# Sparse attention and a mixer: weights loaded ahead of a batch, one batch turned on TensorE, the last tile stored in halves

## The chip, the cores and the metric

One core of a Trainium2 chip runs the whole program. TensorE (PE) multiplies, VectorE (DVE) and ScalarE (ACT) move and transform data, GpSimd (POOL) and SyncE (SP) issue most of the transfers, and ScalarE issues some as well. The metric is the device time of one execution in microseconds (us). It is given as the median of the runs, with the lowest and the highest; the profile is of one more execution.

## The reference

Eight batches, eight heads, 576 positions, 64 numbers a head. Attention is local (32 positions to each side) plus eight global positions that see everything and are seen by everything. Its output goes through a mixer over positions and one over channels.

```python
scores = scale * np.matmul(q, k.transpose(0, 1, 3, 2))
mask = np.abs(pos[:, None] - pos[None, :]) <= window
mask = mask | is_global[:, None] | is_global[None, :]
attn = softmax(np.where(mask, scores, -1e9))
x = np.matmul(attn, v)            # heads side by side: (8, 576, 512)
xt = x.transpose(0, 2, 1)
h = np.maximum(xt @ w_tok1, 0.0) @ w_tok2
u = x + h.transpose(0, 2, 1)
h2 = np.maximum(u @ w_ch1, 0.0) @ w_ch2
return u + h2
```

## The kernel before, in words

**Tiles.** A batch has 576 positions: four full tiles (tau 0 to 3) of 128 and a rest of 64. The rests of an even batch and the odd batch after it share one tile, tau 4. Everything that TensorE reads is float16; it sums into eight banks of float32.

**Steps of one batch b.** The loads of q and k (`load_qk`, L502; their rests `load_rest`, L511) and v (`load_v`, L519) bring float32; casts (`cast_qk` L528, `cast_v` L540) make float16, and `shift_v` (L549) a shifted copy of v, called vod. q and k have to be turned so that the head's 64 numbers lie on partitions: for batches 0 to 2 TensorE does it (`turn_pe`, L560, and `rest_pe`, L581), for batches 3 to 7 a transposing DMA into `raw`, issued by SP, and a VectorE copy out of it (`turn_dma`, L637). `scores` (L658) multiplies, ScalarE takes the exponentials into e, VectorE masks them (L689). The global keys and queries are gathered for four batches at once by indirect DMAs of POOL (`f_gather`, L484) into g_q and g_k, cast and turned in `glob_rows` (L614). `glob_keys`, `glob_sums` and `values` (L696, L715, L731) end in x. `token1` and `token2` (L797, L815) are the mixer over positions, with the result a1 between them; their end is u, added by VectorE at L834 (L837 for the rest, into `ul`). `turn_u` (L840) turns u into uT: for batches 0 to 2 by four transposes of TensorE (L848) and a copy (L850) for each of four tiles, for batches 3 to 7 by a transposing DMA of SP (L853). The shared rest is always turned by a DMA (L843). `chan1` (L862) makes twelve pieces of b1 from wc1 and uT, `chan1l` (L872) the same for the shared rest, `chan2` (L887) multiplies b1 by wc2, in two or three parts of one sum; VectorE adds u at L903 and writes one of three buffers `osb`, and a store takes it to the output (L906 from POOL, or from SP for the last batch; L909 for the shared rest, two stores of 64 rows on SP).

**What sets the order.** No order is written by hand. The program first lists operations with `op`: the engines that may run each with a cost, a priority, what it reads and writes, and for a DMA its work, its packets and its latency. Then `run` (L119) plays the list against these costs: it picks the engine and the operation that can start first, prefers low priorities among those that start close together, and issues the instruction there and then. So the costs and the due times in the code set the order of each engine's instructions, and each engine later works in that order. SP, ACT and POOL have a planned ring of 4096 packets each (L116), and eight semaphores are planned for POOL's transfers and eight for those of SP and ACT together (L131): the ninth transfer of a group waits for the first to land. `warm` (L282) puts multiplications of zeros into planned gaps of TensorE before planned time 34.

**Around the change.** POOL's queue carries, after batch 0: the weights w1 and w2, the gather of g_k, batch 1's q and k, then the channel weights wc1 in three pieces and wc2 in three (`f_wc1` L473, `f_wc2` L479), batch 1's v, all of batch 2, and the second gather. Their priorities stand in L922 to L988. SP's queue carries batch 0, then the loads of batches 3 to 7 between the transposing DMAs; ACT issues v of batches 3 to 7 (L946). Of the last batch, `chan2` for tau 4 comes last of all: two parts of six multiplications of 512 columns, one addition of 512 columns, two stores on SP.

Of the kernel before, what the change touches and what calls it, by code (L numbers as in the profile page):

```python
# [15 lines left out]
P = 128  # L16
# [11 lines left out]
def kernel(  # L28
# [90 lines left out]
    def run(free, look, hop, warm_until):  # L119
# [73 lines left out]
        while ready:  # L193
# [52 lines left out]
            if o["dma"]:  # L246
                work, size, lag, packets = o["dma"]
                q = "A" if e == "K" else e
                drain(min(f, min(free[x] for x in "GSA")))
                f = land(q, f, work, size, i)  # L250
                filled[q].append((f, packets))
                f += lag
                lanes["G" if e == "G" else "S"].append(f)
                f += o["late"] + (LATE if st > 36.0 else 0.3)
# [632 lines left out]
    def chan2(b, tau, pri):  # L887
        i, key = b % 2, ("o", b, tau)
        last = tau == NT - 1
        js = [range(0, 4), range(4, 8), range(8, 12)] if b == 0 else [range(0, 6), range(6, 12)]  # L890
        for part, jr in enumerate(js):
            def f(e, jr=jr):
# [29 lines left out]
    def loads(b, n0=0):  # L922
# [8 lines left out]
            return  # L931
        if b < PEB:
            if b == 1:
                pl = -173.9
            load_rest(b, pl, [("G", 0.73)], [n0] if b == 1 else ())
            for h in range(0, H, 4):
                for ti in range(2):
                    load_qk(b, ti, slice(h, h + 4), pl + 1 + h / 2 if b > 1 else pl + 0.1 + h / 100, [("G", 0.88)], [n0] if b == 1 else ())
            if b > 1:
                load_v(b, pl + 6, [("G", 0.87)])  # L940
        else:
            load_rest(b, pl, [("S", 0.65)])
            for h in range(0, H, 4):
                for ti in range(2):
                    load_qk(b, ti, slice(h, h + 4), pl + 1 + h / 2, [("S", 0.5)])
            load_v(b, pl + 6, [("A", 0.6)])  # L946

    def casts(b):
# [7 lines left out]
    for b in range(B):  # L956
# [17 lines left out]
            op([("G", 0.75)], -16, f_pads2(1), w=[("x", 1, NT - 1), ("lf", 1)])  # L974
        if b < 2:
            for ti in range(2):
                op([("G", 2.7)], (-115 if ti == 0 else -174.2) if b == 0 else 70, f_gather(b, ti), r=["idx"], w=[("g32", b, ti)], dma=(0.1, 256, 1.7, 256), late=0.0 if b or ti else 2.3,
                   behind=[] if b == 0 and ti == 0 else [n2])
        casts(b)
        cast_v(b, ca - 20, [("A", 0.52), ("V", 0.57)] if b < 2 else [("A", 0.52)])  # L980
# [31 lines left out]
        for tau in range(NT):  # L1012
            token2(b, tau, ca + tau)
            if tau < NT - 1 or b % 2:
                turn_u(b, tau, ca + tau + 2, b < 3)
        if b and b % 2 == 0:
            chan2(b - 1, NT - 1, base + 24)
        for j in range(NJ):
# [40 lines left out]
```

## Time and profile before

| | us |
|---|---|
| median of 3 runs | 317.6 |
| lowest and highest of them | 314.32 and 320.36 |
| the profiled execution, its own time | 314.6 |
| its span, first to last instruction | 312.9 |
| TensorE busy in it | 292.0 |
| VectorE, ScalarE, GpSimd busy | 186.8, 180.5, 60.5 |
| mean granted TensorE clock | 0.987 of full speed |

The span leaves out 1.7 us of the profiled execution's time. In the views that the prediction shows, a row of the timeline gives the start in us, the duration, the engine with the line of the code and the tile written and read, how many instructions were merged into it, and in brackets the idle time of that engine just before it and what ended it. A table by stage gives for each stretch the busy time of each engine with its count of instructions, then the granted clock, the share of the DMA engines' time that was busy, and the rate. Ends of matmuls are modelled, so the distance from one start to the next tells more than a duration.

### The profile page before, as it was taken

How to read it: one execution, taken by the hardware profiler on the slowest of the kernel's cores; microseconds unless marked ns; L12 is line 12 of the kernel's file. 1: busy time of each engine (PE TensorE's matmuls, PEld its weight loads, DVE VectorE, ACT ScalarE, POOL GpSimd, SP SyncE). 2: the span in 40 equal slices, each digit the busy share in tenths (PEclk: the TensorE clock that was granted, in tenths of full speed). 3: DMA queues.
4: the chain of work that ended last, by engine and by line, in shares of the span. 5: the costliest groups of instructions: out<-in, count | busy, mean ns of one | idle time of the engine just before them, and what ended most of it. 6: DMA issues, size and time to landing. Idle time of an engine off the chain costs nothing.

```text
span 312.9 us, 7276 instructions
## 1 busy us (share of the span) xinstructions
PE 292.0 (93%) x2943; PEld 154.4 (49%) x2943; DVE 186.8 (60%) x410; ACT 180.5 (58%) x325; POOL 60.5 (19%) x109
## 2 busy tenths in 40 slices
PE   6979889997999979988999998999999999999994
PEld 4755545454474434533456444544555445444641
DVE  7789667569686674876675846964543357230021
ACT  4864895377987758841989376733742083305500
POOL 8589635632001100002000110002000200020000
PEclk9989999999999979999999999999999999999998
DMA  6989999999999999999979999924003211051013
GB/s 183 255 129 287 208 222 222 287 243 234 214 212 220 194 267 318 118 190 221 325 114 176 203 313 189 159 50 136 36 0 63 89 53 37 12 140 69 2 67 102
DMA packets 94660, 51.31 MB, mean 164 GB/s; under 512 B 73698, under 2 KB 89954, under 8 KB 94626
## 3 DMA queue, kind: packets, MB, share of 16 engines
q1 hardware_dynamic: 62480, 26.49, 40.3%
q0 software_dynamic: 8704, 18.45, 24.0%
q10 hardware_dynamic: 23442, 5.90, 11.1%
q8 instruction: 23, 0.38, 0.5%
q14 instruction: 11, 0.09, 0.1%
HBM read 36.11 MB, written 9.44 MB: 146 GB/s over the span
## 4 chain that ended last, share of the span: by engine, by line
PE 58%; DMA 26%; ACT 5%; DVE 5%; issue 2%; SPq 2%; POOL 1%; POOLq 0%; ACTq 0%; DVEq 0%
PE bank L895 22%; PE bank L866 21%; DMA lv<-in_v_dram 8%; DMA raw<-qk 6%; DMA lq<-in_q_dram 5%; PE bank L821 4%; DMA g_q<-in_q_dram,idx_i 3%; PE bank L673 3%; PE bank L803 2%; DMA lk<-in_k_dram 2%; PE bank L878 2%; ACT qk L534 2%; ACT vsh L546 2%; DVE osb L903 2%; PE bank L753 1%
## 5 line engine op out<-in xcount | busy, mean ns | idle before, releaser
L866 PE MATMUL bank<-uT,wc 128*128 128x512 f16 x384 | 94.0, 384 | 6.4 <-DVE osb L903 2.3
L895 PE MATMUL bank<-wc,b 128*128 128x512 f16 x384 | 88.3, 379 | 2.9 <-DVE osb L903 2.2
L858 ACT ACTIVATE b<-bank 128x512 f16<-128x512 f32 x88 | 52.5, 617 | 38.3 <-PE bank L866 38.3
L683 ACT ACTIVATE e<-bank 128x648 f16<-128x648 f32 x64 | 42.7, 737 | 30.0 <-PE bank L673 29.8
L895 PEld LDWEIGHTS <-b 128*128 128x128 f16 x384 | 36.7, 98 | 45.9 <-issue 4.2
L866 PEld LDWEIGHTS <-wc 128*128 128x128 f16 x384 | 35.2, 98 | 48.5 <-issue 8.7
L906 POOL DMA_DIRECT2D out_dram<-osb x28 | 16.1, 574 | 203.1 <-DVE osb L903 203.0
L903 DVE TENSOR_TENSOR osb<-u,bank 128x512 f32<-128x512 f16 x32 | 21.9, 686 | 45.3 <-PE bank L895 41.5
L546 ACT CAST vsh<-lv 128x512 f16<-128x512 f32 (+3 forms) x44 | 26.5, 620 | 9.7 <-DMA uT<-u 5.3
L689 DVE TENSOR_TENSOR e<-e,masku 128x1296 f16<-128x1296 f16 x28 | 23.3, 831 | 13.7 <-ACT e L683 13.2
L834 DVE TENSOR_TENSOR u<-x,bank 128x512 f16<-128x512 f16 x30 | 18.7, 681 | 15.0 <-PE bank L821 14.8
L781 DVE TENSOR_TENSOR x<-bank,rr 128x512 f16<-128x512 f32 x32 | 22.1, 691 | 1.1
L821 PE MATMUL bank<-a,w 128*128 128x512 f16 x80 | 20.1, 379 | 0.5 <-DVE a L809 0.3
L534 ACT CAST qk<-lq 128x512 f16<-128x512 f32 x26 | 16.2, 626 | 4.5 <-DMA lq<-in_q_dram 2.0
L803 PE MATMUL bank<-x,w 128*128 128x512 f16 x64 | 18.7, 379 | 0.0
L673 PEld LDWEIGHTS <-kT 64*128 64x128 f16 x576 | 11.2, 97 | 14.4 <-issue 13.6
L534 ACT CAST qk<-lk 128x512 f16<-128x512 f32 x27 | 16.9, 631 | 1.8 <-DMA lk<-in_k_dram 1.8
L654 DVE COPY qT<-raw 128x512 f16<-128x512 f16 x20 | 12.0, 602 | 7.2 <-DMA raw<-qk 7.1
L753 PEld LDWEIGHTS <-e 128*64 128x64 f16 x576 | 16.1, 116 | 0.1
L740 PE MATMUL bank<-rf,lf 128*64 128x264 f16 x144 | 15.6, 293 | 0.5 <-DVE rf L726 0.5
L753 PE MATMUL bank<-vsh,e 128*64 128x66 f16 x320 | 16.0, 199 | 0.0
L673 PE MATMUL bank<-qT,kT 64*128 64x72 f16 x576 | 15.4, 198 | 0.0
(164 smaller groups left out, 333.6 us busy)
## 6 DMA issues: line engine op xcount, KB each, us to landing
out_dram<-osb POOLq DMA_DIRECT2D x28, 256.0 KB, 4.3
lq<-in_q_dram SPq DMA_DIRECT2D x11, 512.0 KB, 6.4
lk<-in_k_dram SPq DMA_DIRECT2D x11, 512.0 KB, 7.9
lv<-in_v_dram ACTq DMA_DIRECT2D x15, 256.0 KB, 4.6
wc<-in_moe_w_ch_dram POOLq DMA_DIRECT2D x6, 512.0 KB, 12.8
lq<-in_q_dram POOLq DMA_DIRECT2D x4, 512.0 KB, 6.4
lk<-in_k_dram POOLq DMA_DIRECT2D x4, 512.0 KB, 11.0
lv<-in_v_dram ACTq DMA_DIRECT2D x10, 192.0 KB, 3.8
```

What stands on the lines that cost most here:

```text
L534: COPY[e](out=qk[:, ti, p].rearrange("q i (r d) -> q r i d", r=2), in_=(lq, lk)[ti][:, hs])
L546: COPY[e](out=vsh[i][a:z, c, :, 0:D], in_=lv[a:z, c])
L673: nc.tensor.matmul(ps_tile[keys[z]][:, u // 3, UW * (u % 3) : UW * (u % 3) + UW], lhsT=kT[r, 64 * u : 64 * u + P], rhs=qT[r, u // 2, UW * ...
L683: op([("A", 0.595)], pri + 1, lambda e, par=par: nc.scalar.activation(out=es[i][:, 2 * p + par].rearrange("p (n u) x -> p n u x", n=3), in ...
L689: op([("V", 0.85)], pri + 2, lambda e: nc.vector.tensor_mul(out=e2, in0=e2, in1=masku.unsqueeze(1).to_broadcast([P, 2, NB, UW])), r=["mask ...
L753: nc.tensor.matmul(o[:, VW * hh : VW * hh + VW], lhsT=es[i][:, h, 2 * tau + c, x : x + 64], rhs=vod[i][:, tau, h, :] if c else vsh[i][:, t ...
L803: nc.tensor.matmul(ps_tile[key][:, tt], lhsT=w, rhs=x16s[i][:, ch, :], start=(ch == 0), stop=(ch == NT - 1))
L821: nc.tensor.matmul(ps_tile[key], lhsT=w2[:, ch, P * tau - sh : P * tau - sh + P], rhs=a1[:, ch, :], start=(ch == 0), stop=(ch == 1 and not ...
L858: nc.scalar.activation(out=out, in_=in_, func=AF.Relu)
L866: nc.tensor.matmul(ps_tile[key], lhsT=wc1[:, cc, P * j : P * j + P], rhs=uT[:, cc, :], start=(cc == 0), stop=(cc == 3))
L895: nc.tensor.matmul(ps_tile[key], lhsT=w, rhs=wc2[:, j, :], start=(j == 0), stop=(j == NJ - 1))
L903: nc.vector.tensor_add(out=osb, in0=uls[b // 2 % 2] if last else u16s[i][:, tau], in1=ps_tile[key])
```

## The change

Four edits. The three pieces of wc1 go into POOL's queue ahead of the gather of g_k and of batch 1's q and k, by new priorities. u of batch 3 is turned by TensorE, as in batches 0 to 2. The last tile of all is computed in two halves of 256 columns, each in its own bank, with its own addition and two stores, one issued by SP and one by ScalarE. And the planner changes: a transfer that ScalarE issues now also occupies SP in the plan, by 0.9 us for each 1024 packets, and a load of q or k of batches 3 to 7 is planned to hold SP for 1.15 instead of 0.5.

```diff
@@ in run, where a DMA is issued
             if o["dma"]:
                 work, size, lag, packets = o["dma"]
                 q = "A" if e == "K" else e
+                if e == "A":
+                    free["S"] = max(free["S"], st) + 0.9 * o["dma"][3] / 1024
@@ chan2
+        if last and b == B - 1:
+            osb = osbs[nout[0] % 3]
+            for z in range(2):
+                cs, kz = slice(256 * z, 256 * z + 256), ("o", b, tau, z)
+                def f(e, cs=cs, kz=kz):
+                    for j in range(NJ):
+                        nc.tensor.matmul(ps_tile[kz], lhsT=b1l[:, j, :], rhs=wc2[:, j, cs], start=(j == 0), stop=(j == NJ - 1))
+                op([("P", 1.31)], pri + z, f, r=[("wc2", t) for t in range(3)] + [("b1l", t) for t in range(3)], ps=[kz], new=("M", [kz], [P, 256], F32))
+                op([("V", 0.4)], pri - 8, lambda e, cs=cs, kz=kz: nc.vector.tensor_add(out=osb[:, cs], in0=uls[b // 2 % 2][:, cs], in1=ps_tile[kz]),
+                   r=[("ul", b // 2 % 2, 0), ("ul", b // 2 % 2, 1)] + ([] if z else [("osb", nout[0] % 3)]), ps=[kz], w=[("osbz", z)])
+                for y in range(2):
+                    op([("SA"[y], 0.45)], pri + 5 + z, lambda e, y=y, cs=cs: ENG[e].dma_start(
+                        out=out[b - 1 + y, S - LAST : S, cs], in_=osb[64 * y : 64 * y + 64, cs]), r=[("osbz", z)], dma=(0.25, 1024, 0.8, 64))
+            return
@@ loads
             if b == 1:
-                pl = -173.9
+                pl = -170.9
...
-                    load_qk(b, ti, slice(h, h + 4), pl + 1 + h / 2, [("S", 0.5)])
+                    load_qk(b, ti, slice(h, h + 4), pl + 1 + h / 2, [("S", 1.15)])
@@ the gathers
-                op([("G", 2.7)], (-115 if ti == 0 else -174.2) if b == 0 else 70, f_gather(b, ti), ...
+                op([("G", 2.7)], (-115 if ti == 0 else -170.95) if b == 0 else 70, f_gather(b, ti), ...
@@ the loop over batches
-                turn_u(b, tau, ca + tau + 2, b < 3)
+                turn_u(b, tau, ca + tau + 2, b < 4)
```

Because the planner replays everything, these edits move instructions of all engines from 18 us on to the third batch. The lines below carry the line numbers of the changed kernel in its own rows (two higher up to L889, sixteen higher after it).

POOL, after the load of w2 (`w`); wc is a piece of wc1 or wc2, lr, lq, lk, lv are the landing buffers of the rests, of q, k and v. Before:

```order
L471 DMA w_107<-in_moe_w_tok_dram 128x2x576
L487 DMA g_k_193<-in_k_dram,idx_i 128x64 x2
L514 DMA lr<-in_q_dram 64x8x64
L514 DMA lr<-in_k_dram 64x8x64
L504 DMA lq<-in_q_dram 128x4x256
L504 DMA lk<-in_k_dram 128x4x256
L504 DMA lq<-in_q_dram 128x4x256
L504 DMA lk<-in_k_dram 128x4x256
L474 DMA wc_108<-in_moe_w_ch_dram 128x4x512 x3
L480 DMA wc_109<-in_moe_w_ch_dram 128x4x512
L523 DMA lv<-in_v_dram 96x8x64
```

POOL at the same place, changed:

```order
L473 DMA w_107<-in_moe_w_tok_dram 128x2x576
L476 DMA wc_108<-in_moe_w_ch_dram 128x4x512 x3
L489 DMA g_k_193<-in_k_dram,idx_i 128x64 x2
L516 DMA lr<-in_q_dram 64x8x64
L516 DMA lr<-in_k_dram 64x8x64
L506 DMA lq<-in_q_dram 128x4x256
L506 DMA lk<-in_k_dram 128x4x256
L506 DMA lq<-in_q_dram 128x4x256
```

The three pieces of wc1 stand ahead of the gather of g_k and of batch 1's q and k; the first piece of wc2 and batch 1's v still follow all of these.

VectorE at the end of batch 1's mixer over positions: u is batch 1's sum, osb the output tiles of batch 0, g_q the second gather. Before:

```order
L534 CAST qk<-lk 128x2x4x64
L834 TENSOR_TENSOR u_1_95<-x_1_92,bank 128x512 x4
L903 TENSOR_TENSOR osb_102<-u_0_94,bank 128x512
L837 TENSOR_TENSOR ul_96<-x_1_92,bank 64x512
L617 CAST g_q_196<-g_q_192 128x128
L554 COPY vod_78<-vsh_76 64x2112
L903 TENSOR_TENSOR osb_103<-u_0_94,bank 128x512
```

VectorE there, changed:

```order
L536 CAST qk<-lk 128x2x4x64
L919 TENSOR_TENSOR osb_102<-u_0_94,bank 128x512
L619 CAST g_q_196<-g_q_192 128x128
L919 TENSOR_TENSOR osb_103<-u_0_94,bank 128x512
L836 TENSOR_TENSOR u_1_95<-x_1_92,bank 128x512 x4
L839 TENSOR_TENSOR ul_96<-x_1_92,bank 64x512
```

The cast of g_q, which waits for the gather, stood behind the four additions of u and now stands ahead of them. On ScalarE the cast of g_k likewise moved: it stood behind all four copies of batch 1's uT (L850) and now stands ahead of all four (L852).

VectorE at the end of batch 2's mixer over positions: u_0 and ul are batch 2's sums, raw and rawr hold the turned q and k of batch 4, osb the output tiles of batch 1. Before:

```order
L834 TENSOR_TENSOR u_0_94<-x_0_91,bank 128x512 x4
L837 TENSOR_TENSOR ul_97<-x_0_91,bank 64x512
L646 COPY qT_72<-rawr 128x4x64
L648 COPY kT_74<-rawr 128x4x64
L903 TENSOR_TENSOR osb_104<-u_1_95,bank 128x512
L654 COPY qT_72<-raw 128x4x128
L903 TENSOR_TENSOR osb_102<-u_1_95,bank 128x512
L651 COPY kT_74<-raw 128x512
L654 COPY qT_72<-raw 128x4x128
L651 COPY kT_74<-raw 128x512
L654 COPY qT_72<-raw 128x4x128
L903 TENSOR_TENSOR osb_103<-u_1_95,bank 128x512
```

VectorE there, changed:

```order
L836 TENSOR_TENSOR u_0_94<-x_0_91,bank 128x512 x4
L839 TENSOR_TENSOR ul_97<-x_0_91,bank 64x512
L919 TENSOR_TENSOR osb_104<-u_1_95,bank 128x512
L556 COPY vod_78<-vsh_76 64x2112 x2
L919 TENSOR_TENSOR osb_102<-u_1_95,bank 128x512
L919 TENSOR_TENSOR osb_103<-u_1_95,bank 128x512
L691 TENSOR_TENSOR e_81<-e_81,masku 128x1296
```

Six copies out of raw and rawr, each behind a transposing DMA, stood among the additions into osb; they now come later, behind and between the masked exponentials of batch 3. From batch 4's scores on, TensorE's order is the same in both kernels up to the last tile.

More of the change, by code (lines that the diff above doesn't have):

```diff
@@ L976 @@
             for ti in range(2):
-                op([("G", 2.7)], (-115 if ti == 0 else -174.2) if b == 0 else 70, f_gather(b, ti), r=["idx"], w=[("g32", b, ti)], dma=(0.1, 256, 1.7, 256), late=0.0 if b or ti else 2.3,
+                op([("G", 2.7)], (-115 if ti == 0 else -170.95) if b == 0 else 70, f_gather(b, ti), r=["idx"], w=[("g32", b, ti)], dma=(0.1, 256, 1.7, 256), late=0.0 if b or ti else 2.3,
                    behind=[] if b == 0 and ti == 0 else [n2])
```

## The prediction

> **What bounds the kernel now.** First the page: how much of the span is TensorE.
>
> ```profile
> span 312.9 us, 7276 instructions
> PE 292.0 (93%) x2943; PEld 154.4 (49%) x2943; DVE 186.8 (60%) x410; ACT 180.5 (58%) x325; POOL 60.5 (19%) x109
> ```
>
> TensorE is busy for 93% and no other engine for more than 60%, so the time is TensorE's work and TensorE's idle time. Where the idle time lies, the table by stage tells (busy us of PE, PEld, DVE, ACT, POOL, granted clock, DMA share, rate):
>
> ```profile
> 30.00:77.00 47.00, 42.15 (x454) 23.10 (x453) 32.66 (x65) 32.66 (x60) 22.61 (x32) 1.00 1.18 244
> 77.00:145.00 68.00, 63.25 (x640) 32.01 (x639) 48.38 (x101) 48.79 (x89) 3.19 (x5) 0.97 1.08 213
> 145.00:200.00 55.00, 53.73 (x615) 28.04 (x614) 37.20 (x78) 40.37 (x75) 4.09 (x7) 1.00 1.05 219
> 200.00:308.20 108.20, 108.18 (x903) 54.08 (x901) 43.63 (x81) 40.92 (x70) 6.48 (x12) 1.00 0.22 63
> ```
>
> From 200 to 308 TensorE never stops and the DMA engines are at 22%; nothing but less work helps there. Up to 200 the DMA engines are full (105 to 118%) and TensorE idles 4.85, 4.75 and 1.27 us, 10.9 in all. From 308.2 to the end of the span, 312.9, comes a tail of 4.7 us without TensorE. So the change can win at most those 10.9 us, what a low clock cost on top, and part of the tail. The table of waits names what ended TensorE's (us in total, times, longest):
>
> ```profile
> PE bank L866 <- DVE osb L903: 2.3, 2, 2.1
> PE bank L895 <- DVE osb L903: 2.2, 2, 1.8
> PE bank L720 <- DVE eg L692: 1.9, 2, 1.0
> ...
> PE bank L866 <- ACT b L858: 1.1, 1, 1.1
> ```
>
> None of these is a transfer. VectorE and ScalarE work in order, and had stood still behind an instruction that waited for a transfer, as the next parts show. The change moves such instructions.
>
> **Weights first, up to 77 us.** What POOL and the DMA engines did before, and who waited:
>
> ```profile
> 17.92 0.72 POOL L471 DMA_DIRECT2D w<-in_moe_w_tok_dram  x1
> 25.96 2.33 POOL L474 DMA_DIRECT2D wc<-in_moe_w_ch_dram  x3
> 22.00:26.00 4.00, 4.00 (x73) 3.38 (x68) 3.12 (x9) 0.87 (x2) 4.00 (x7) 0.68 0.60 146
> 32.29 0.39 PE L848 MATMUL bank<-ident,u 128*128 128x128 f16 x4
> 36.08 1.90 PE L866 MATMUL bank<-uT,wc 128*128 128x512 f16 x8 [1.28 <-DMA wc<-in_moe_w_ch_dram]
> 38.54 0.77 POOL L480 DMA_DIRECT2D wc<-in_moe_w_ch_dram  x1 [1.14 <-DMA wc<-in_moe_w_ch_dram]
> 41.08 0.75 POOL L480 DMA_DIRECT2D wc<-in_moe_w_ch_dram  x1 [1.77 <-DMA wc<-in_moe_w_ch_dram]
> 44.86 1.25 ACT L546 CAST vsh<-lv 32x512 f16<-32x512 f32 x2 [0.65 <-DMA lv<-in_v_dram]
> ```
>
> wc1 is now issued right behind w2, at 18.6 instead of 25.96, into DMA engines that idled 40% of the 4 us from 22 to 26: 1.6 us are filled, and whatever follows all of these transfers lands 1.6 us earlier. The wait of 1.28 goes. `chan1` of batch 0 can start when u is turned and copied, about 32.9 (32.29, the transposes and a copy), 3.2 us earlier; but 38 transposes of batch 1 and of the gather, which stood ahead of it, now come after its start, 2.1 us at the 56 ns of the L878 row below: 1.1 us gained.
>
> Then something else is late. Batch 1's q and k come behind three pieces of wc1, each 2.5 us (the distance of the two POOL rows, each of which waited for an earlier piece to land): 7.5 less 1.6, or 5.9 us later. Their casts and turns now fall between the pieces of `chan1`, on ScalarE and VectorE. ScalarE's row has the first cast of v as early as behind batch 1's first exponentials; v can land at 44.8 less 1.6, at 43.2. Behind that cast stand, in ScalarE's new order, two casts, six exponentials, two short ones and four pieces of b1: at the spacing of such rows in the profile
>
> ```profile
> 46.62 1.31 ACT L683 ACTIVATE e<-bank 128x648 f16<-128x648 f32 x2
> 50.00 1.07 ACT L858 ACTIVATE b<-bank 128x512 f16<-128x512 f32 x2
> 50.32 0.47 PE L720 MATMUL bank<-vsh,eg 128*32 128x132 f16 x20
> ```
>
> some 8.3 us, so b1 is whole at about 51.5, then a part of `chan2` (0.87) and `glob_sums`, which began at 50.32 before. The second part of `chan2` that is done ahead counts in favour and what waited for rf is covered: 0.6 us behind, the 1.1 spent. The wait for b of 1.1 was of this kind before, behind the row at 44.86.
>
> Next the second gather. These rows show it (the first is from the chain of waits):
>
> ```profile
> 61.38 8.22 DMA g_q<-in_q_dram,idx_i
> 63.43 2.48 DVE L834 TENSOR_TENSOR u<-x,bank 128x512 f16<-128x512 f16 x4
> 69.69 0.23 DVE L617 CAST g_q<-g_q 128x128 f16<-128x128 f32 x1 [2.06 <-DMA g_q<-in_q_dram,idx_i]
> 71.98 0.30 ACT L617 CAST g_k<-g_k 128x128 f16<-128x128 f32 x1 [2.24 <-DMA g_k<-in_k_dram,idx_i]
> 73.30 1.02 PE L866 MATMUL bank<-uT,wc 128*128 128x512 f16 x4 [1.62 <-DVE qT L589]
> ```
>
> VectorE added u of batch 1 at 63.4 and only then waited for g_q. Now g_q's cast stands ahead of u; it can start at 69.6 less 1.6, at 68.0, so u starts near 68.9, and ScalarE's copies of uT stand behind g_k, near 70.3. Queued behind them are TensorE's transposes of u and all of `chan1` of batch 1, and on SP the turn of the shared rest with the loads behind it. TensorE has two parts of `chan2` and batch 2's turns to do meanwhile, which is why 5.5 us on VectorE shrink to about 0.9 us behind at 77.
>
> A wait also costs clock here. Before, it did so at 113:
>
> ```profile
> 113.27 1.85 PE L866 MATMUL bank<-uT,wc 128*128 128x512 f16 x4 [2.08 <-DVE osb L903]
> 112.00:118.00 6.00, 4.73 (x30) 1.76 (x29) 5.77 (x11) 2.80 (x5) 0.54 (x1) 0.72 0.97 255
> ```
>
> After a wait of 2.08 us the granted clock was 0.72 over 6 us: 1.7 us of TensorE's time. The waits of 1.62 and 1.28 brought no such fall. The front now has two places with waits of 2 to 3 us (about 49 and 67); I count one fall at even odds, 0.8. Front: 0.9 + 0.8 = **1.7 us slower**. Its bounds: 4.8 faster, if all idle time of the stage goes; 5.9 slower, if the gathers are no earlier than before (the 0.9 and the 1.6 not gained, 2.5) and the clock falls twice (3.4).
>
> The Trainium skill (TensorE: Matmul & The Clock Gate, What's actually happening) has the clock fall after an idle window of about 3.4 us. By that rule the front's waits, each shorter, cost no clock, and the sum below would be 0.8 less. The row at 113 does not agree: 2.08 us idle were enough there; the measurement decides.
>
> **The planner's new rule, 77 to 200 us.** The long wait ended by VectorE at 113 is made by this:
>
> ```profile
> 112.03 0.59 DVE L654 COPY qT<-raw 128x512 f16<-128x512 f16 x1 [1.25 <-DMA raw<-qk]
> 112.54 0.68 DVE L903 TENSOR_TENSOR osb<-u,bank 128x512 f32<-128x512 f16 x1
> 134.75 0.61 DVE L654 COPY qT<-raw 128x512 f16<-128x512 f16 x1 [2.50 <-DMA raw<-qk]
> 137.96 2.48 DVE L834 TENSOR_TENSOR u<-x,bank 128x512 f16<-128x512 f16 x4
> 141.94 4.26 PE L895 MATMUL bank<-wc,b 128*128 128x512 f16 x19 [1.78 <-DVE osb L903]
> ```
>
> osb, which frees a bank, stood behind copies of batch 4's raw, which waited for transposing DMAs; at 142 osb stood behind u of batch 3, and u behind copies of batch 5's raw. In the changed order osb and u stand ahead of these copies at both places. So the waits of 2.1 and 1.8 lose their cause, and with the first the 1.7 of clock. The wait of 1.0 for eg was of the same kind. Together 6.6 us. But raw is still needed, SP issues batch 3's eight transposes later than before, and each copy that moved stands ahead of something else. I let four tenths come back: **4.0 us faster**; bounds 7.7 faster (all idle time of both stages and the clock) and 3.8 slower (none goes, and one wait with its clock is added).
>
> **u of batch 3 on TensorE.** Sixteen transposes. The chain's row for four, its row for 48 other matmuls of 128 columns, and the copies:
>
> ```profile
> 101.63 0.32 PE bank L848 x4
> 292.54 2.69 PE bank L878 x48
> L850 ACT COPY uT<-bank 128x512 f16<-128x512 f16 x11 | 6.3, 589 | 2.4 <-PE bank L848 2.3
> ```
>
> Ends are modelled, so a short row reads too long; over 48 in a row one takes 56 ns, and sixteen take **0.9 us**, on the path, because TensorE has work everywhere from there. Where it would have waited anyway they cost nothing: bounds 0 to 1.3 (four times 0.32). Four copies of 0.59 go to ScalarE and VectorE, which idle over a quarter of that stage, and four DMAs leave SP; I count nothing for either. If that cover is gone, the copies cost up to 2.4, inside the bound above.
>
> **The last tile.** The addition of 256 columns, the old end, and the landing times of the stores at L909:
>
> ```profile
> 26.44 0.86 DVE L789 TENSOR_TENSOR x<-bank,rr 64x256 f16<-64x256 f32 x2
> 308.22 0.69 DVE L903 TENSOR_TENSOR osb<-ul,bank 128x512 f32<-128x512 f16 x1 [1.90 <-PE bank L895]
> 308.93 1.12 SPq L909 DMA_DIRECT2D out_dram<-osb  x2
> DMA to landing us min/median/max: 2.2/3.7/5.5
> ```
>
> The last addition has 256 columns, 0.43 instead of 0.69: 0.27. Its two stores go out side by side, so the second no longer waits half of 1.12: 0.56. The first half's addition and stores lie beside the second half's multiplications. Together 0.8, and a smaller transfer may land a little sooner: **0.9 us faster**; bounds 0 (if transfers of 1 KB rows take longer by as much) to 1.4. Twice as many multiplications of half the columns I take as the same time for TensorE.
>
> **Sum.** 1.7 − 4.0 + 0.9 − 0.9 = −2.3, so 312.3 against the profiled execution's own 314.6 (span 312.9 and 1.7 around it). The median shown, 317.6, lies 3.0 above that execution, which is near the lowest run. A new median should fall between; I add half of the 3.0: **313.8**, 1.2% under the median. Two per cent, 6.4 us, the spread of the three runs, is about what a measurement of this kernel can tell from no change.
>
> **Rivals**, each with the same 1.5 added:
>
> *The plan holds.* In the front the 1.1 of the first step and the waits of 1.1 for b and 1.6 for qT count, 3.8 gained, and all 6.6 go later: with 0.9 and −0.9, −10.4, 305.7. For it: every long wait has its cause moved. Against: 8.3 us of ScalarE behind v, and g_q ahead of u.
>
> *The gather decides.* g_q and g_k ahead of batch 1's u and uT: if they land when they did (69.6 and 71.9), the front loses 2.5 and the clock falls twice, 5.9; of the later gain half is left, −2.0: +3.9, 320.0, slower than before. It takes over from the forecast when g_q lands later than about 69. For it: in the profile every engine that waits for the gather stands idle 2 us. Against: the DMA engines' idle 1.6 us are really filled.
>
> *The waits change place.* The DMA engines are as full as before, and idle time only moves: 0 + 0 + 0.9 − 0.9, 316.1.
>
> **Chances.** Forecast 0.55, plan holds 0.20, gather decides 0.17, waits change place 0.08. Below 311.2, faster by over 2%: most of the second and the lower edge of the first, 0.22. Above 324: the upper edge of the third, 0.05. Between: 0.73. Range 308.0 to 320.0: it takes the forecast's own bounds of some 5 us down and 6 up, and leaves out most of the second and half of the third.
>
> **What would show it.** Right: no wait of TensorE for wc; TensorE 0.5 to 2 us later than before at batch 2's `glob_keys`; VectorE idle ahead of g_q's cast; no wait over 1.5 us for osb between 105 and 145 and clock 1.00 there; sixteen more transposes of u at 56 ns; the tail 0.9 us shorter. The forecast is wrong if the front is level or ahead at 77, or if waits for osb of 2 us remain.

## The result and the profile after

| | before | after |
|---|---|---|
| median, us | 315.96 (313.7 to 320.36, 4 runs) | 330.08 (327.98 to 331.87, 4 runs) |
| ratio, with its 95% interval | | 1.0469 (1.0353 to 1.0586) |
| the profiled execution, its own time and its span | 314.6 and 312.9 | 327.98 and 326.3 |
| mean granted TensorE clock | 0.987 | 0.979 |

The change made the kernel 14 to 15 us slower; the forecast was 313.8 with a range to 320.0. Medians here and below count every run; the ratios and their intervals leave out runs more than 1.5% above the fastest of their kernel. The head of the page after, and the table by stage (busy us of PE, PEld, DVE, ACT, POOL, granted clock, DMA share, rate):

```profile
span 326.3 us, 7336 instructions
PE 294.6 (90%) x2968; PEld 156.2 (48%) x2968; DVE 187.3 (57%) x409; ACT 183.3 (56%) x331; POOL 59.0 (18%) x109
```

```profile
30.00:77.00 47.00, 40.21 (x420) 21.90 (x418) 29.37 (x61) 31.01 (x56) 24.18 (x36) 1.00 1.12 267
77.00:145.00 68.00, 59.35 (x638) 30.57 (x639) 43.84 (x92) 49.59 (x93) 2.45 (x4) 0.95 0.82 172
145.00:200.00 55.00, 50.51 (x475) 25.88 (x475) 35.97 (x67) 32.31 (x60) 4.32 (x8) 0.97 0.93 194
```

TensorE is busy 2.6 us longer (at half clock it is busy too), yet for a smaller share of the span. It idles 6.8, 8.7 and 4.5 us where it idled 4.9, 4.8 and 1.3, and the DMA engines are less busy than before (82% and 93% for 108% and 105%): they are not what has become short. The table of waits names the new ones, first TensorE's and then ScalarE's:

```profile
PE bank L823 <- ACT a L814: 8.6, 2, 4.3
PE bank L675 <- ACT kT L576: 4.1, 1, 4.1
ACT a L814 <- DMA lv<-in_v_dram: 6.6, 1, 6.6
```

The first two rows are three waits of 4.1 to 4.3 us, all ended by ScalarE; the waits for osb of 2.1 and 1.8 us are gone (1.3 is the longest now). Here they are in TensorE's timeline, and the clock over the 6 us at each:

```profile
79.47 0.47 PE L675 MATMUL bank<-qT,kT 64*128 64x72 f16 x18 [4.07 <-ACT kT L576]
83.11 0.63 PE L705 MATMUL bank<-qT,kgz 128*32 128x512 f16 x4
110.00 1.42 PE L823 MATMUL bank<-a,w 128*128 128x512 f16 x5 [4.34 <-ACT a L814]
147.39 1.70 PE L823 MATMUL bank<-a,w 128*128 128x512 f16 x6 [4.23 <-ACT a L814]
```

```profile
80.00:86.00 6.00, 6.00 (x43) 2.11 (x42) 3.75 (x8) 5.24 (x12) 0.00 (x0) 0.72 0.45 62
110.00:116.00 6.00, 6.00 (x32) 3.14 (x32) 3.32 (x6) 4.02 (x7) 0.00 (x0) 0.72 1.23 270
147.00:153.00 6.00, 5.61 (x28) 3.01 (x28) 3.78 (x6) 4.49 (x9) 0.00 (x0) 0.72 0.44 73
```

Each cost 1.7 us of clock on top, 28% of 6 us: 6 us at each of three places. (Before, the clock fell once in this stretch, at 113.) Row L705 is `glob_keys` of batch 2; it stood at 76.14 before, so TensorE is 7.0 us behind there. What ScalarE did instead is in its own timeline (rows ACTq are its DMA issues):

```profile
67.08 0.94 ACTq L525 DMA_DIRECT2D lv<-in_v_dram  x2
70.01 0.30 ACT L619 CAST g_k<-g_k 128x128 f16<-128x128 f32 x1 [2.32 <-DMA g_k<-in_k_dram,idx_i]
70.09 2.21 ACTq L525 DMA_DIRECT2D lv<-in_v_dram  x1
72.34 0.59 ACT L852 COPY uT<-bank 128x512 f16<-128x512 f16 x1 [2.03 <-PE bank L850]
72.50 3.93 ACTq L525 DMA_DIRECT2D lv<-in_v_dram  x1
76.53 1.07 ACT L852 COPY uT<-bank 128x512 f16<-128x512 f16 x2 [3.12 <-issue]
```

Batch 3's loads of v (L525) stand among batch 1's copies of uT. The third and the fourth took 2.2 and 3.9 us to issue, and the copies of uT and kT waited behind them. Before, two loads stood there, and each took 0.4 us:

```profile
69.18 0.35 ACTq L523 DMA_DIRECT2D lv<-in_v_dram  x1
72.08 0.40 ACTq L523 DMA_DIRECT2D lv<-in_v_dram  x1
```

Near 105 us the chain of waits tells what such a load itself stands at (start, us, what):

```profile
102.50 5.93 DMA lq<-in_q_dram
...
108.50 0.38 ACTq L525
...
108.92 1.03 ACT a L814
```

SP issued a load of q at 102.5; it lands at 108.4, and only then is ScalarE's fourth load of v issued, which uses the same semaphore again. a, a relu, waits behind it, and TensorE for a until 110.00. ScalarE's queue at this place, before:

```
L531 CAST rn<-lr 128x512
L534 CAST qk<-lq 128x2x4x64
L546 CAST vsh_77<-lv 96x8x64
L534 CAST qk<-lk 128x2x4x64
L534 CAST qk<-lq 128x2x4x64
L812 ACTIVATE a_93<-bank 128x1024
```

and changed:

```
L533 CAST rn<-lr 128x512
L525 DMA lv<-in_v_dram 96x8x64
L525 DMA lv<-in_v_dram 128x8x64 x3
L814 ACTIVATE a_93<-bank 128x1024
L525 DMA lv<-in_v_dram 96x8x64
```

Near 142 it is the same with three loads of batch 5's v; one of them is issued as k lands, 7.18 us after SP issued k.

```profile
136.68 7.18 DMA lk<-in_k_dram
...
143.88 0.38 ACTq L525
```

### The profile page after: what moved, and what is told of

Same layout as the page of the kernel before. It is cut to its first block, busy times and chain, and to the rows that moved or that the text cites. A ratio compares the mean times of both kernels' runs of the same rounds, so it can differ in the third digit from the quotient of the medians.

```text
span 326.3 us, 7336 instructions
## 1 busy us (share of the span) xinstructions
PE 294.6 (90%) x2968; PEld 156.2 (48%) x2968; DVE 187.3 (57%) x409; ACT 183.3 (56%) x331; POOL 59.0 (18%) x109
## 4 chain that ended last, share of the span: by engine, by line
PE 60%; ACT 6%; DMA 5%; issue 2%; DVE 2%; ACTq 1%; SPq 0%; DVEq 0%
PE bank L911 22%; PE bank L868 21%; PE bank L823 4%; PE bank L675 3%; DMA lk<-in_k_dram 2%; PE bank L805 2%; DMA lq<-in_q_dram 2%; ACT qk L536 2%; PE bank L880 2%; ACT vsh L548 2%; DMA raw<-qk 1%; PE bank L742 1%; PE bank L755 1%; ACT b L860 1%; PE bank L850 1%
## 5 line engine op out<-in xcount | busy, mean ns | idle before, releaser
L823 PE MATMUL bank<-a,w 128*128 128x512 f16 x80 | 22.6, 413 | 9.9 <-ACT a L814 8.6
L536 ACT CAST qk<-lq 128x512 f16<-128x512 f32 x29 | 17.8, 639 | 3.0 <-DMA lq<-in_q_dram 3.0
L823 PEld LDWEIGHTS <-w 128*128 128x128 f16 x80 | 7.9, 103 | 18.1 <-issue 11.4
```

Of the source, the lines that this page charges most:

```text
L536: COPY[e](out=qk[:, ti, p].rearrange("q i (r d) -> q r i d", r=2), in_=(lq, lk)[ti][:, hs])
L823: nc.tensor.matmul(ps_tile[key], lhsT=w2[:, ch, P * tau - sh : P * tau - sh + P], rhs=a1[:, ch, :], start=(ch == 0), stop=(ch == 1 and not ...
```

## The experiments

Theory A: ScalarE stands at its own loads of v, and what is queued behind them is late. Theory B: the weights ahead of batch 1 make all data late. Theory C: the transfers are late whatever stands in ScalarE's queue. The table has all eighteen runs: the median, the ratio to the kernel before on the same chip with its interval, and how far TensorE's start was behind before's (minus: ahead) in the profiled execution at `glob_keys` of batch 2 (76.14 before), at the first `token2` of batch 2 (100.17), at `glob_keys` of batch 4 (149.41) and at `chan1` of batch 7 (280.72).

| run | us | ratio | keys 2 | token2 2 | keys 4 | chan1 7 |
|---|---|---|---|---|---|---|
| the change | 330.08 | 1.0469 (1.0353 to 1.0586) | 7.0 | 9.8 | 14.5 | 13.7 |
| e1 rule alone | 313.01 | 0.9954 (0.9915 to 0.9993) | -0.1 | -0.7 | -2.8 | -3.6 |
| e2 weights alone | 322.31 | 1.0247 (1.0211 to 1.0283) | 5.6 | 4.7 | 5.8 | 7.6 |
| e3 u and tail | 317.36 | 1.0081 (1.0036 to 1.0125) | 0.9 | 1.6 | 0.0 | 2.0 |
| e15 u alone | 318.49 | 1.0104 (1.0056 to 1.0152) | 0.0 | 0.0 | 0.5 | -0.4 |
| e8 rule and tail | 311.81 | 0.9917 (0.9875 to 0.9958) | 0.5 | -0.1 | 0.7 | 0.8 |
| e7 rule and weights | 332.67 | 1.0599 (1.0504 to 1.0694) | 6.4 | 8.7 | 16.2 | 17.7 |
| e4 change, loads held in the plan | 319.62 | 1.0137 (1.0070 to 1.0204) | 2.0 | 1.1 | 4.8 | 7.4 |
| e5 change, loads on POOL | 325.67 | 1.0354 (1.0259 to 1.0448) | 5.9 | 7.6 | 9.7 | 12.3 |
| e6 weights, loads on POOL | 328.56 | 1.0470 (1.0377 to 1.0563) | 5.5 | 6.2 | 7.5 | 12.9 |
| e9 change, kT first | 325.00 | 1.0268 (1.0154 to 1.0382) | 1.8 | 4.6 | 10.1 | 10.4 |
| e10 change, a first | 333.86 | 1.0586 (1.0499 to 1.0673) | 8.5 | 6.7 | 19.9 | 20.6 |
| e11 both | 326.81 | 1.0299 (1.0186 to 1.0412) | 2.2 | 0.8 | 14.9 | 13.9 |
| e13 change, all first | 324.27 | 1.0281 (1.0197 to 1.0365) | 2.2 | 0.8 | -0.5 | 10.2 |
| e18 change, all late | 321.55 | 1.0257 (1.0193 to 1.0321) | 1.9 | 0.5 | -1.0 | 7.2 |
| e12 rule, tail, held in the plan | 326.79 | 1.0375 (1.0285 to 1.0465) | -0.9 | -2.7 | 4.9 | 12.3 |
| e14 rule, tail, all first | 324.23 | 1.0302 (1.0231 to 1.0373) | -0.1 | -0.7 | -7.1 | 10.7 |
| e17 rule, tail, all late | 321.51 | 1.0244 (1.0193 to 1.0294) | 0.1 | -0.5 | -7.0 | 7.9 |
| e16 before, all first | 318.63 | 1.0149 (1.0057 to 1.0241) | -0.3 | -0.3 | -4.7 | 3.8 |

In the rows below, line numbers are those of each kernel, whose added lines move them.

**The edits apart.** e1, e2 and e3 have one or two of the four edits each, word for word as in the diff above: e1 the lines in `run` and the 1.15, e2 the two priorities, e3 `turn_u` and the tail.

> The kernel before with the planner's new rule alone (ScalarE's transfers also hold SP in the plan, 1.15 instead of 0.5 for a load of q or k). In ScalarE's order three loads of batch 4's v then stand ahead of the a of batch 2, and a fourth and fifth right behind it; before, none stood there. Theory A (ScalarE stands at its own loads of v, and what is queued behind them is late): a wait of TensorE of 2 to 4.5 us for a at token2 of batch 2, near 100 us, with a fall of the clock (1.7 us), while the 2.1 and 1.7 that the kernel before lost at 113 may go: 314 to 320 us, 317 the likeliest. Theory B (the weights ahead of batch 1 make everything late, the planner's rule is good as I had forecast): no such wait, 309 to 313. Theory C (the transfers are late whatever stands in ScalarE's order): as before, 314 to 316.

The rule alone is 0.5% faster and 3.6 us ahead in its profile, at the top of what theory B gave. Theory A missed: the third of three loads ahead of a was issued at 97.77, and a was hardly late.

```profile
98.20 1.02 ACT L814 ACTIVATE a<-bank 128x1024 f16<-128x1024 f32 x1 [1.43 <-DMA raw<-qk]
```

So a load in the queue need not cost anything. It cost where the transfer whose semaphore it needs was late (near 105 and 142 in the change) and where its issue was long (near 70).

> The kernel before with the weights wc1 ahead of the gather and of batch 1's q and k, and nothing else of the change. In ScalarE's order four loads of batch 3's v stand among g_k and batch 1's copies of uT, ahead of batch 2's kT (two before), and two loads of batch 4's v ahead of the a of batch 2 (none before). Theory A: TensorE waits some 4 us for kT near 75 and 1 to 2.5 us for a near 105, with one clock fall or two: 6 to 10 us more than before, 321 to 325. Theory B: the front alone makes all of the loss, 326 to 331. Theory C: 2 to 4 us more than before, 317 to 319.

As theory A has it near 75: 5.6 us lost by `glob_keys` of batch 2, most of it one wait. The wait for a near 105 that it also named did not come (4.7 behind at `token2`, no further back).

```profile
71.77 3.79 ACTq L523 DMA_DIRECT2D lv<-in_v_dram  x1
78.60 0.47 PE L673 MATMUL bank<-qT,kT 64*128 64x72 f16 x18 [3.92 <-ACT kT L574]
```

> The kernel before with u of batch 3 turned by TensorE and the last tile in two halves, without the other two edits. No load of v comes to stand ahead of an a that had none before. All theories: 0.9 slower and 0.9 faster, so the same as before within 1.5 us, about 315; the end of TensorE's work to the end of the span 0.3 to 0.9 us shorter than 4.7.

Slower by 0.8%, 1 to 4 us by the interval, more than the sum had; its tail, from the start of the last addition to the end of the span, takes 4.2 us instead of 4.7, as expected. e15 asked where the rest goes.

> The kernel before with u of batch 3 turned by TensorE alone. By my sum 0.9 slower, 315.4; by the run with the tail (0.8% slower in all, the tail some 0.4 faster) about 3 slower, 317.5, with the wait of 2.6 us for u near 135 that stood in that run's profile.

u alone is 1.0% slower, 1.8 to 4.8 us. Its profile has the wait for u:

```profile
136.74 0.61 PE L848 MATMUL bank<-ident,u 128*128 128x128 f16 x4 [2.87 <-DVE u L834]
```

But this profiled execution (314.78) is one of the lowest of ten and is level with before's at the end, so it does not show where the median's 3 us lie.

> The planner's rule and the last tile in halves, without the other two edits. All theories: as the rule alone, less 0.4 to 0.9 for the tail, 312.3; from the end of TensorE's work to the end of the span 4.3 instead of 4.7. Should the rule's gain of 3.6 us in its profile not be one of the rule but of a lucky execution, 314.

0.8% faster than before, the best version found (the profiled execution, 314.4, is its slowest of ten, hence the 0.8 behind in the table). From the start of the last addition to the end of the span it takes 3.6 us here (309.08 to 312.7), 4.3 in the changed kernel (321.97 to 326.3), and took 4.7 before.

> The planner's rule and weights first together, without the other two edits. ScalarE's order has four loads of batch 4's v ahead of the a of batch 2, as in the changed kernel; the rule alone had three, weights alone two, and neither made TensorE wait there. Theory A, with the point that the loads block only when the transfers of SP ahead of them have not landed: a wait of about 4.5 us for a near 105 and the clock's fall, 324 to 330. A rival, that the edits' times simply add (1.2 faster and 8.1 slower): 321, and no wait over 2 us there.

The times don't add: 332.7 where adding gives 321. With the weights ahead the four loads meet a late q, and a comes 6 us late; the rule, harmless alone, is what put four loads there. TensorE waited 3.8 for a, without the clock's fall that was expected. The time is 2.7 above theory A's range, and the longest wait is at a third place, 7.9 us for osb at 159.4: ScalarE stands at four loads of v, and a cast, VectorE's shift and osb stand behind them.

```profile
107.79 1.02 ACT L814 ACTIVATE a<-bank 128x1024 f16<-128x1024 f32 x1 [6.10 <-DMA lv<-in_v_dram]
146.13 11.15 ACTq L525 DMA_DIRECT2D lv<-in_v_dram  x4
```

**The loads out of the way: planned anew.** e4 holds them back in the plan (the lines that fill `held` are left out):

```diff
-            load_v(b, pl + 6, [("A", 0.6)])
+            hold_v = {3: ("kT", 2), 4: ("uT", 2), 5: ("uT", 3)}.get(b)
+            load_v(b, pl + 6, [("A", 0.6)], [held[hold_v]] if hold_v in held else ())
```

> The changed kernel, with one thing more: in the plan ScalarE's loads of v are held behind a copy of its own, those of batch 3 behind the last copy into kT of batch 2, those of batch 4 behind the last copy into uT of batch 2, those of batch 5 behind the last copy into uT of batch 3. So no load of v stands ahead of these on ScalarE. Theory A: the three waits of 4.2 to 4.5 us for kT and a go, and the three clock falls of 1.7 us behind them: 18 us less than the 330 of the changed kernel at the most, 312 to 318. Theory B: the front stays 3 to 7 us behind, the later waits are then those of late data: 323 to 329. Theory C: no change, 328 to 331.

10 us less than the changed kernel, but 1.6 above theory A's range. The waits near 75 and 105 are gone (2.0 and 1.1 behind). What is left is the same thing elsewhere: five loads held so long come in one row, ScalarE stands 9 us, and batch 4's exponentials wait.

```profile
140.86 9.23 ACTq L526 DMA_DIRECT2D lv<-in_v_dram  x5
152.84 1.31 ACT L686 ACTIVATE e<-bank 128x648 f16<-128x648 f32 x2 [1.47 <-issue]
```

In e5 and e6 POOL issues these loads: `[("G", 0.87)]` for `[("A", 0.6)]` in the same line.

> The changed kernel with the loads of v of batches 3 to 7 issued by POOL, so that ScalarE's queue holds no load of v at all; the planner replays everything. Theory A (ScalarE stands at its own loads, waiting for older transfers to land, and kT, a and the exponentials queued behind them are late): no wait of TensorE over 1.5 us for kT, a or e between 70 and 165, glob_keys of batch 2 about 2 us behind before instead of 7, in all 312 to 318. Theory B (weights first makes all late, and late data make the waits): 324 to 330. Theory C (the transfers are late whoever issues them): 327 to 331.

> Weights first alone, as in the run that took 322.3, with the loads of v of batches 3 to 7 issued by POOL. Theory A: the wait of 3.9 us for kT near 75 goes, with the fall of the clock behind it; what stays are the three waits of about 1 us at 43, 49 and 51, so glob_keys of batch 2 is 2 to 3 us behind before, not 5.6: 314 to 319. Theory B: glob_keys as late as without it, 320 to 325.

Both miss theory A: no load of v stands on ScalarE, and e5 wins 4 us, within what theory B gave, while e6 is 6 us slower than e2 and above both theories. At `glob_keys` of batch 2 they are 5.9 and 5.5 behind: the plan now puts casts of batch 3's v, which wait for their load, among the copies of uT, and TensorE waits 2.0 and 2.2 us for kT, again with a fall of the clock. Later VectorE stands at copies out of raw and rawr, as it did before the change, and osb waits behind them. VectorE and then TensorE in e6:

```profile
119.63 0.23 DVE L646 COPY qT<-rawr 128x256 f16<-128x256 f16 x1 [7.54 <-DMA rawr<-rn]
119.91 1.28 DVE L903 TENSOR_TENSOR osb<-u,bank 128x512 f32<-128x512 f16 x2
120.64 1.87 PE L866 MATMUL bank<-uT,wc 128*128 128x512 f16 x4 [3.58 <-DVE osb L903]
```

A kernel that is planned anew changes more than the thing in question. So the next ones keep the plan and move instructions in ScalarE's queue alone.

**The loads out of the way: the plan kept.** e9; a held instruction is issued when the one named is (the lines that fill `mark` are left out, other cuts are marked):

```diff
-            o["fn"](e)
+            if hold_for.get(i) and mark[hold_for[i]] not in done:
+                waiting.setdefault(mark[hold_for[i]], []).append((o["fn"], e))
+            else:
+                o["fn"](e)
+            done.add(i)
+            for fn, en in waiting.pop(i, []):
+                fn(en)
...
+                hold_for[z] = {(3, 2): ("chan1", 1, 2), (3, 3): ("chan1", 1, 5)}.get((b, z - first))
```

> The changed kernel with two of ScalarE's instructions moved and nothing planned anew: its third and fourth load of batch 3's v, which stood among the copies of batch 1's uT and took 2.2 and 3.9 us to issue, go behind two pieces of b1 of batch 1. Theory A (ScalarE stands at its own loads): the copies of uT and kT come at once, TensorE's wait of 4.1 us for kT near 75 shrinks to 1 or less, the fall of the clock behind it (1.7) goes, glob_keys of batch 2 is 2 us behind before, not 7; the waits near 105 and 142 stay: 324 to 326. The finding with the loads on POOL speaks for a rival, that kT is late by its data anyway: wait 2 to 4, 328 to 331.

Theory A. Two instructions moved, 5 us won in the median and as much at `glob_keys` of batch 2; the copies of uT start at 70.39 and the wait for kT is 0.87 instead of 4.07.

```profile
70.39 1.06 ACT L860 COPY uT<-bank 128x512 f16<-128x512 f16 x2
75.67 0.47 PE L683 MATMUL bank<-qT,kT 64*128 64x72 f16 x18 [0.87 <-ACT kT L584]
```

e10 holds batch 4's loads 0 to 3 behind `("a1", 2)` in the same way, e11 does both.

> The changed kernel with one instruction of ScalarE moved and nothing planned anew: the a of batch 2 goes ahead of the four loads of batch 4's v instead of behind them. Theory A: TensorE's wait of 4.5 us for a near 105 and the fall of the clock behind it go: 6 less than the changed kernel, 323 to 325. Rival: the copies of uT behind the loads are then what is late, and TensorE waits as long for chan1 of batch 2: 328 to 331.

> Both moves together. Theory A: they add, 10 to 12 less than the changed kernel, 317 to 320, with glob_keys of batch 3 some 3 us behind before instead of 12. Rival (what is saved at one place is waited for at the next): 322 to 330.

The rival was right on the place: in e10 a comes at once, but the copies of uT and TensorE's next transposes then stand behind the same loads, and longer, so that 333.9 is above even the rival's 331. The same holds for e11, whose 326.8 is the rival's too. The rows are e10's:

```profile
105.74 1.02 ACT L822 ACTIVATE a<-bank 128x1024 f16<-128x1024 f32 x1 [2.11 <-PE bank L813]
105.80 10.26 ACTq L533 DMA_DIRECT2D lv<-in_v_dram  x5
118.49 0.59 PE L858 MATMUL bank<-ident,u 128*128 128x128 f16 x4 [7.25 <-ACT uT L860]
```

So e13 moves ScalarE's loads and casts of v past what TensorE had been seen to wait for, one at a time; VectorE's shifts of v follow the casts. The places: (uT, batch, tile), (a1, batch), (e, batch, pair of heads), (b1, batch, piece).

```
loads of batch 3, pieces 2 and 3:  (b1, 1, 2), (b1, 1, 5)
loads of batch 4:  (uT, 2, 3), (e, 3, 1), (e, 3, 3), (b1, 2, 1), (b1, 2, 3);  casts:  (b1, 2, 5) to (b1, 2, 9)
loads of b = 5, 6, 7:  (a1, b-2), (e, b-1, 1), (e, b-1, 3), (b1, b-2, 1), (b1, b-2, 3);  casts:  (b1, b-2, 5) to (b1, b-2, 9)
```

> The changed kernel, planned as it is, with ScalarE's loads and casts of v alone put elsewhere in its queue (VectorE's shifts of v follow the casts): two loads of batch 3 behind pieces of b1 of batch 1; of batches 4 to 7 the first load behind the copies of uT (batch 4) or the a of two batches before, two more among the exponentials and two among the pieces of b1, each alone, and the casts one by one behind later pieces of b1. Theory A (ScalarE standing at its loads is what cost the time): no wait of TensorE over 2 us from 70 to 165, glob_keys of batch 3 at most 4 us behind before, in all 316 to 320. Theory C (the data are late whatever the queue): waits of 4 us for a, uT or e remain, 325 to 331.

Up to 149 us all that was lost is back, though the end of 316 to 320 that theory A gave is missed: `token2` of batch 2 starts without a wait at 101.01, and `glob_keys` of batch 4 at 148.92, where the change had 163.89 and before 149.41.

```profile
148.92 0.41 PE L719 MATMUL bank<-qT,kgz 128*32 128x512 f16 x4
```

After that it loses 10 us, at places that I had chosen for batch 5. e18 has others: loads of b = 5 to 7 at (b1, b-2, 0), 2, 4, 6 and 8, casts at (b1, b-2, 10), 11 and behind (a1, b-1).

> The whole change with ScalarE's loads and casts of v placed in that way, those of batch 3 as before. Theory A: level with before at glob_keys of batch 4, and to the end within 3 us: 313 to 318, so that all but 3 of the changed kernel's 14 us were ScalarE's loads. Rival (something else of the change is late from 150 on): 321 to 328.

Level with before at the same place again (148.44), and 2.5 behind at 202 us instead of 10. Then it loses 5 more up to `chan1` of batch 7, so theory A's end time of 313 to 318 is missed, and the time is the rival's (321 to 328). What is late from there, though, is at least in part of the run's own making: VectorE's shift of batch 6's v stands 4.17 us for ScalarE's casts, which e18 places behind the a of batch 5; u and osb stand behind the shift, and TensorE waits for osb.

```profile
209.60 1.44 DVE L570 COPY vod<-vsh 64x2112 f16<-64x2112 f16 x2 [4.17 <-ACT vsh L562]
216.19 5.34 PE L925 MATMUL bank<-wc,b 128*128 128x512 f16 x24 [1.78 <-DVE osb L933]
```

Theory C falls with e9, where two moved instructions won 5 us with the same transfers; theory B is left with the 2 us by which e9, e13 and e18 are still behind at `glob_keys` of batch 2.

**Looking for a faster version.** e12 is e8 with batch 4's loads held in the plan as in e4; e14 and e17 are e8 with the places of e13 and e18 (batch 3's untouched); e16 is the kernel before with those of e13 for batches 4 to 7.

> The planner's rule and the tail in halves, as in the run of 311.8, with the loads of batch 4's v held in the plan behind the last copy into uT of batch 2. In that run TensorE still lost some 5 us at batch 3's scores between 107 and 113, to copies and exponentials that stood behind these loads on ScalarE. Theory A: those waits go, 306 to 310. Rival: the loads are as long in the way at the next place, as where they were held in the whole change (4.4 us near 149): 311 to 316.

> The planner's rule and the tail in halves (311.8), with the loads and casts of v of batches 4 to 7 put elsewhere in ScalarE's queue in the same way. Theory A: the 5 us that TensorE lost between 107 and 113 go, 306 to 310. Rival (as when the loads were held in the plan: 326.8): ScalarE stands longer at one of the new places, 314 to 327.

> The planner's rule and the tail in halves, with ScalarE's loads and casts of batch 4's v placed as in the run of 324.2, which was 7.1 us ahead of before at glob_keys of batch 4; the loads of v of batches 5 to 7 now stand one by one among the pieces of b1 of two batches before, behind SP's burst of transposing transfers, and their casts at the end of these pieces and behind the next a. Theory A: the lead of 7 stays, 305 to 309. Rival: ScalarE's loads cost at any place, 314 to 324.

> Control: the kernel before with the loads and casts of v of batches 4 to 7 put elsewhere in ScalarE's queue in the same way. Its ScalarE lost little to its loads; theory A: within 2 us of before, 312 to 316. If it is 3 or more faster, the move gains whatever the change does, and what e14 gains is not the rule's.

All are slower than e8. Theory A missed four times; in e14 and e17 the time is the rival's, and e12 is 11 us above its rival's 316. e14 and e17 were 7 us ahead at `glob_keys` of batch 4, and lost 15 to 18 from there. The first 6 to 7 of it go where a load of batch 5's v stands behind SP's transposing transfers (raw), and what follows it on ScalarE waits. So it is in e14, the first row; the second and third are ScalarE and TensorE of e12, where VectorE's shift of v waits for ScalarE's cast in turn and holds osb and TensorE:

```profile
148.55 0.60 ACT L724 ACTIVATE lf<-bank 128x512 f16<-128x512 f32 x1 [4.87 <-DMA raw<-qk]
```

```profile
145.55 0.62 ACT L549 CAST vsh<-lv 128x512 f16<-128x512 f32 x1 [7.01 <-DMA raw<-qk]
154.34 0.63 PE L706 MATMUL bank<-qT,kgz 128*32 128x512 f16 x4 [9.14 <-DVE osb L920]
```

The control e16 was 4.7 us ahead at that place and 3.8 behind at the end: the early places win something in the kernel before too, and the later ones lose more. Some 4 of its 8.5 us are clock: from 158.6 to 168.8 it was granted half, with TensorE busy for 7.7 of these 10.2 us. So 4.7 of what e13 won up to 149 us, and most of e14's 7, are not the change's.

## Why the prediction was wrong

**The step that failed** is in the prediction's part on the front (up to 77 us): "ScalarE's copies of uT stand behind g_k, near 70.3. Queued behind them are TensorE's transposes of u and all of `chan1` of batch 1". Two loads of v stood ahead of g_k, a third ahead of these copies and a fourth among them, and the sum had no term for a load that ScalarE issues: the prediction followed ScalarE's casts and copies, and of the transfers only POOL's and SP's. The same omission is in the planner's term: "In the changed order osb and u stand ahead of these copies at both places. So the waits of 2.1 and 1.8 lose their cause." They did, and at both places a load of v on ScalarE made a wait of 4.3 instead. How much it is, e13 and its control tell, by one profiled execution each: with these loads and casts moved (and the shifts that follow them), 14.5 us behind at 149 becomes 0.5 ahead; the same move, batch 3's loads apart, puts the kernel before 4.7 ahead. With ScalarE's queue cleared in both, the change is thus 4.2 behind (2 of it already at `glob_keys` of batch 2), and some 10 of the 14.5 are what it did to that queue. From 149 on the change loses no more. Whether all 10 could be kept to the end is not settled: both sets of places that I tried lost 8 to 11 us between there and the end, at least in part to the moved loads and casts themselves.

Point by point:

- *Weights first, 1.7 slower.* The wait of 1.3 for wc went ("None of these is a transfer" was true only of the rows that the prediction shows of its table of waits); `chan1` started at 33.30, 2.8 earlier (3.2 foretold). g_q's cast began at 68.22 and u at 68.95, as foretold (68.0 and 68.9). The copies of uT, foretold for 70.3, began at 72.34 and stopped again at 72.5; with the two loads moved they began at 70.39. Batch 1 was 2.6 behind at `glob_sums`, not 0.6: three waits of 0.5 to 1.0 us in place of one.

```profile
33.30 1.02 PE L868 MATMUL bank<-uT,wc 128*128 128x512 f16 x4 [0.25 <-ACT uT L852]
44.27 1.02 PE L868 MATMUL bank<-uT,wc 128*128 128x512 f16 x4 [0.96 <-DVE qT L571]
50.22 1.02 PE L868 MATMUL bank<-uT,wc 128*128 128x512 f16 x4 [0.55 <-ACT b L860]
52.96 0.65 PE L722 MATMUL bank<-vsh,eg 128*32 128x132 f16 x20 [0.85 <-DVE e L691]
68.22 0.23 DVE L619 CAST g_q<-g_q 128x128 f16<-128x128 f32 x1 [1.85 <-DMA g_q<-in_q_dram,idx_i]
68.95 2.47 DVE L836 TENSOR_TENSOR u<-x,bank 128x512 f16<-128x512 f16 x4
```

  Without the loads in the way (e9) TensorE was 1.8 behind at `glob_keys` of batch 2, near the term; with them 7.0, above its bound of 5.9. Alone the edit costs 2.5%, 8 us. Which of its two moves does this, the gather or batch 1's q and k, was not tried.
- *The planner's rule, 4.0 faster.* Alone it is 3.6 ahead in the profile, but that execution is one of its fastest; by the ratio it is 0.5% faster, 1.4 us (0.2 to 2.7). Right on the waits for osb, nearly three times too high on the size. It doesn't add to the first edit: together they are 6.0% slower.
- *u of batch 3, 0.9.* Mis-sized: 3.3 (1.8 to 4.8) alone. I costed the transposes and no wait, and called 2.4 us for uncovered copies inside a bound that ended at 1.3. TensorE waits 2.4 (e3) and 2.9 us (e15) for u; where the median's loss goes is open.
- *The tail, 0.9.* 0.4 in the change, by the start of the last addition and the end of the span; 0.5 in e3, 1.1 in e8. Inside the bounds.
- *The clock.* Counted as a fall at even odds in the front and none later. There were three falls, 5.1 us, one behind each wait of ScalarE's making, where before had one.
- *The rivals.* "The waits change place" had the mechanism, with a chance of 0.08, but took the idle time as given; it grew by 9 us. "The gather decides" was rightly turned down: g_q landed before 69. None had a price above 320, since all three were built from waits that the profile before contained.
- *What would show it.* The signs of failure that I named (a front level or ahead, waits for osb of 2 us) did not come, and the forecast failed all the same. Of the signs of being right, "0.5 to 2 us later" at batch 2's `glob_keys` failed (7.0) and so did "clock 1.00 there" (0.72).

## What to carry to other kernels

When a plan or a scheduler moves instructions, read every engine's new queue for DMA issues too, and ask of each what it waits for (the landing of an older transfer, whose semaphore it uses again) and which compute stands behind it: here a load issued early on an engine that computes was cheap only while the older transfers were on time. Edits that are planned together don't add: try them alone and in pairs, and to test a cause move the suspected instruction alone, without planning anew. Price a wait of TensorE with its clock: here 4.3 us cost 6.

## What the runs showed of the hardware

- The issue of a load can itself take long: 2.2 and 3.9 us for the third and the fourth in a row on ScalarE (72.50 to 76.43), where the first two together took 0.9. The timeline calls the wait behind it issue. The first of the four, of 192 KB, landed 9.1 us after its issue at 67.08, at 76.2, just before the fourth was through; that a full ring of descriptors holds the issue fits this, and was not tried (SP's own issue beside it, 1.31 us from 72.18, ended too early to be all of it). The Trainium skill (DMA: Bandwidth & Descriptors, Issuing engines are not separate DMA queues) says that issuing from several engines only saves the sequencer's time, which it calls usually small beside the transfer; here an issue of 3.9 us stood beside a transfer of 9.1.

```profile
lv<-in_v_dram ACTq DMA_DIRECT2D x1, 192.0 KB, 9.1
```

- In the traces of before, after and the eighteen runs, TensorE had 17 waits of 3.9 us or more by the timeline's brackets; with each of them went 3.4 us or more at half the clock (3.4 at the three places above, up to 20.5 from 147.5 in e12). Between 2.0 and 3.8 us it went either way: the 2.1 before the change brought a fall, 2.4 us in e3 at 137.4 and 3.8 in e7 at 108.9 did not. The clock fell behind several short waits too: in e16 TensorE was busy for 2.8 of the 6 us from 156 to 162, with no wait over 1.4, and the granted clock was 0.50 from 158.6 to 168.8. The Trainium skill (TensorE: Matmul & The Clock Gate, What's actually happening) gives an idle window of about 3.4 us for the fall; the waits of 3.9 us and more agree with it; the 2.1 before the change shows that less can do, and the 3.8 in e7 that a little more than 3.4 need not.
